# The row sums of a sliding-window softmax issued directly behind their exponential, with the filler units behind them

## The chip, the cores and the metric

The kernel runs on one core of one Trainium2 chip. The metric is device time in microseconds (us); lower is better. A core has five engines that work side by side, each through its own instructions in the order in which they were issued: PE multiplies matrices into PSUM, the accumulators; ACT evaluates functions element by element and here also moves most PSUM results to SBUF (an eviction); DVE does elementwise arithmetic; POOL and SP mostly start transfers. An engine that waits holds up all that is queued behind.

## The reference, cut to what matters

Two independent computations, put side by side in the output. Part A is attention in which each of 2048 positions sees only eight others (itself and every second one of the 15 before it), with 32 heads of 18 channels:

```python
qkv = (x @ wqkv).reshape(B, S, 3, H, Dh)           # S = 2048, H = 32, Dh = 18
idx = pos[:, None] - arange(8)[None, :] * 2        # eight keys for each position
logits = einsum("bhsd,bhswd->bhsw", q, kg) * Dh ** -0.5
logits = where(idx >= 0, logits, -1e9)
attn = softmax(logits, axis=-1)                    # over the eight
o = einsum("bhsw,bhswd->bhsd", attn, vg)
a = o.reshape(B, S, D) @ wo                        # D = 576
```

Part B is a long causal convolution over the 2048 positions for each of 576 channels (in the reference by FFT), of a four-tap filtered `k` times `v`, gated by `q`:

```python
kv = k_shift * v
y = irfft(rfft(pad(kv)) * rfft(pad(ssm_k)))[:S] + kv * ssm_D
b = q * y
out = concatenate([a, b], axis=-1)
```

## The kernel before, in words

Part B is computed as block transforms with matrices of sines and cosines on PE: `mirror` and `fold_filter` prepare blocks, `filter_spectrum` (tile `ps_fk`, lines 627 and 628, evicted by ACT at line 695) transforms the filter, `x_spectrum` (`ps_fx`, line 776, evicted at 778) the signal, and `spectral` multiplies spectra on DVE (line 1099), sums them (`ps_z`, line 1126) and transforms back (`ps_inv`, `ps_back`).

Part A projects `x` to q, k and v (`project`, tile `ps_proj`: lines 378, 382 and 389 on PE, evicted at line 414), in units that are cut in two halves of four matmuls with 512 columns and, in one of the halves, two or four shorter ones at line 382 or 389. `logits` forms products q times k on DVE (line 832) and sums each head's channels on PE (`ps_log`, line 847). `softmax` treats one half of the positions at a time, `hh` 0 and 1, over a tile `at` of 128 partitions and 8 x 256 elements. `weigh` then multiplies by v on DVE (line 956; three buffers take turns, two halves of `av` and a stretch of `qk`) and sums the eight terms on PE with an identity (`ps_acc`, lines 973 and 987), evicted at lines 977 and 991. `output` multiplies by wo (`ps_wo`, lines 1021 and 1029).

PSUM is used as four double banks: two under tag A, two under tag B. A matmul that starts a new tile waits until ACT has evicted the one that used the bank before.

One pass of `softmax` has these steps: maximum over the eight on DVE (lines 875 to 878), subtraction (879), the exponential of all 128 x 2048 elements on ACT (881), the sum over the eight on PE by eight matmuls with the identity into `ps_tot` (887), the reciprocal on ACT as exp(-ln(sum)) (888 and 889), and the multiplication by it on DVE (892). It is a Python generator. Between its yields the caller issues steps of others, so the yields fix what is issued in between on every engine.

Independent PE work lies in a list, `units`. `until()` takes from it the next number in the table `PLACES` and issues so many units at that point of the program; these are the fillers. The sequence of calls to `until()` pairs each call with its number. In the pass for `hh` 0 the call at line 884 issues one unit of `filter_spectrum`; in the pass for `hh` 1 it issues three half units of the v projection, 16 matmuls. The call at line 880 stands ahead of the exponential. The line numbers 885 to 889 of before are lower by one in the changed kernel: 886 is the sum, 887 the logarithm, 888 the second exponential.

Of the kernel before, what the change touches and what calls it, by code (L numbers as in the profile page):

```python
# [53 lines left out]
def view(t, offset, dims):  # L54

    return bass.AP(tensor=t.tensor, offset=t.offset + offset, ap=[list(t.ap[0])] + [list(d) for d in dims])
# [3 lines left out]
def kernel(  # L60
# [58 lines left out]
    def bank2(name, tag):  # L119
        return pp.tile([128, 2, 512], FP32, name=name, tag=tag)  # L120
# [206 lines left out]
    def dve(n, fn, ready=0.0, ns=0.53):  # L327

        fn()
        clk["D"] = max(clk["D"], ready) + n * ns / 1000 + 0.125  # L330
        return clk["D"]

    def pe(us, tag, evac, ready=0.0, first=True, last=True):

        clk["P"] = max(clk["P"], ready, psum[tag].popleft() if first else 0.0) + us
        clk["A"] = max(clk["A"], clk["P"] + 0.1) + evac
        if last:
            psum[tag].append(clk["A"])
        return clk["A"]

    def pop(n=0):
        f = units[n][1]
        del units[n]
        f()
# [3 lines left out]
    def until():  # L348

        for _ in range(next(places, 0)):  # L350
            if units:
                p = max(clk["P"], psum["A"][0] if psum["A"] else 0.0)
                pop(next((n for n, u in enumerate(units) if len(u) < 4 or u[3] <= p), 0))
# [511 lines left out]
    def softmax(hh, big, small):  # L865

        at = attn[hh]
        t4 = view(big, 0, [[256, 4], [1, 256]])
        t2 = view(small, 0, [[256, 2], [1, 256]])
        top = view(big, 0, [[1, 256]])  # L870
        total = view(big, 0, [[1, 512]]).bitcast(FP32)
        part = view(small, 0, [[1, 256]])
        tt = nc.vector.tensor_tensor
        if hh == 0:
            dve(128, lambda: tt(at[0:32, :, 0:PAD], at[0:32, :, 0:PAD], maskb[:], ALU.add), clk["A"])
        dve(1024, lambda: tt(t4, at[:, 0:4, :], at[:, 4:8, :], ALU.max), clk["A"])
        dve(512, lambda: tt(t2, t4[:, 0:2, :], t4[:, 2:4, :], ALU.max))
        dve(256, lambda: tt(top, t2[:, 0, :], t2[:, 1, :], ALU.max))
        r = dve(2048, lambda: tt(at, at, top.unsqueeze(1).to_broadcast([128, W, 256]), ALU.subtract))
        until()  # L880
        nc.scalar.activation(at, at, ACT.Exp, scale=SCALE)
        clk["A"] = max(clk["A"], r) + 1.9
        yield clk["A"]
        until()
        ps = bank2("ps_tot", "B")
        for w in range(W):
            nc.tensor.matmul(ps[:, 0, 0:256], ident[:], at[:, w, :], start=(w == 0), stop=(w == W - 1))
        nc.scalar.activation(total, ps[:, 0, 0:256], ACT.Ln)
        nc.scalar.activation(part, total, ACT.Exp, scale=-1.0)
        pe(0.85, "B", 0.75, clk["A"])  # L890
        yield clk["A"]
        r = dve(2048, lambda: tt(at, at, part.unsqueeze(1).to_broadcast([128, W, 256]), ALU.mult), clk["A"])
        yield r
# [13 lines left out]
    la, lb = logits(0), logits(1)  # L907
    logits_run[0] = True
    sa = softmax(0, view(av, 2048, [[1, 1024]]), view(av, 3072, [[1, 512]]))
    order = [la] * 3 + [partial(negate, 1, 0)] + [la] * 7 + [lb, sa, lb, lb, lb, sa, lb, sa]  # L910
    for n, step in enumerate(order):
# [3 lines left out]
        step() if callable(step) else next(step, None)  # L915
    need("fk0")
    sb_ = softmax(1, view(xw, 11 * HB + D, [[1, 1024]]), view(xw, 11 * HB + D + 1024, [[1, 512]]))


# [426 lines left out]
```

## Time and profile before

| | |
|---|---|
| time before, median of 3 runs (lowest to highest) | 212.2 us (212.09 to 212.56) |
| the profiled execution | 212.5 us |
| its span, first to last instruction | 210.8 us |
| busy: PE, DVE, ACT, POOL | 200.1, 193.1, 150.5, 74.0 us |
| mean granted clock of PE | 0.998 of full speed |

The profile comes from one execution. A row of the view in order of time has the start in us from the span's start, the duration, the engine, the source line, the operation, out<-in by the program's names, the shape, and how many instructions the row holds; in square brackets stand the engine's idle time just before it and what ended it ("issue" where nothing shown did). A row of the chain of waits has start, duration, engine, tile and line. A row by stretches has the stretch, its length, busy us and number of instructions of PE, weight loads, DVE, ACT and POOL, the granted clock, the share of the transfer engines and GB/s. A few matmul records can be missing.

### The profile page before, as it was taken

Reading aid. Unit: us, or ns where it says so; the run is one execution under the profiler, and the core shown is the slowest. Engines: PE = TensorE matmul, PEld = TensorE weight load, DVE = VectorE, ACT = ScalarE, POOL = GpSimd, SP = SyncE. Lnnn points to the kernel's source line nnn. Section 1 sums busy time; section 2 is a strip of 40 time slices with the busy share of each in tenths; the row PEclk is TensorE's granted clock in tenths of the full one; section 3 lists DMA queues with packets and bytes.
Section 4 is the critical chain, followed back from the end, with each engine's and each line's share of the span. In section 5 each row is a group of like instructions: output and inputs, shape, how many; then the busy total and the mean of one; then the engine's idle time right before and its main releaser. Section 6 shows DMA issues by size and latency. Waiting matters only on the chain.

```text
span 210.8 us, 5106 instructions
## 1 busy us (share of the span) xinstructions
PE 200.1 (95%) x2114; PEld 110.7 (53%) x2122; DVE 193.1 (92%) x146; ACT 150.5 (71%) x218; POOL 74.0 (35%) x111
## 2 busy tenths in 40 slices
PE   7999999999999999899999999999989999999891
PEld 2443443344554656564354666656555666666460
DVE  7989999999999999858889999999999849999981
ACT  3799988657684989986369788855666796775540
POOL 8999993001195516320175000002029004033000
PEclk9999999999999999999999999999999999999999
DMA  6999998999639336999999997587559995985133
GB/s 201 303 328 231 266 342 280 170 192 182 151 75 122 48 40 87 180 181 171 235 225 238 194 234 159 105 208 185 153 223 255 239 322 110 214 243 182 28 113 111
DMA packets 35396, 39.66 MB, mean 188 GB/s; under 512 B 17619, under 2 KB 29007, under 8 KB 35374
## 3 DMA queue, kind: packets, MB, share of 16 engines
q1 hardware_dynamic: 26812, 24.88, 47.2%
q0 software_dynamic: 6096, 11.96, 30.4%
q10 hardware_dynamic: 2466, 2.51, 3.5%
q8 instruction: 16, 0.26, 0.5%
q14 instruction: 6, 0.05, 0.1%
HBM read 13.11 MB, written 4.72 MB: 85 GB/s over the span
## 4 chain that ended last, share of the span: by engine, by line
PE 80%; ACT 10%; DVE 5%; issue 2%; DVEq 0%; ACTq 0%
PE ps_proj L378 16%; PE ps_z L1126 9%; PE ps_wo L1029 8%; PE ps_acc L973 7%; PE ps_inv L1158 7%; PE ps_fx L776 6%; PE ps_log L847 4%; PE ps_proj L500 3%; PE ps_fk L627 3%; PE ps_proj L382 3%; PE ps_proj L389 3%; ACT Ks L695 3%; PE ps_rev L673 2%; PE ps_fk L628 1%; ACT qk L977 1%
## 5 line engine op out<-in xcount | busy, mean ns | idle before, releaser
L378 PE MATMUL ps_proj<-xw 128*128 128x512 bf16 x153 | 37.4, 380 | 0.6 <-issue 0.3
L832 DVE TENSOR_TENSOR av<-qk 128x4096 bf16<-128x4096 bf16 (+1 forms) x16 | 31.7, 2013 | 2.8 <-PE ps_log L847 2.8
L378 PEld LDWEIGHTS <-xw 128*128 128x128 bf16 x160 | 14.0, 97 | 20.5 <-issue 6.2
L1099 DVE TENSOR_TENSOR qk<-xw,Ks 128x2304 bf16<-128x2304 bf16 x14 | 18.5, 1355 | 2.5 <-PE ps_inv L1158 2.4
L1139 ACT ACTIVATE av<-ps_z 128x768 bf16<-128x768 f32 x20 | 15.3, 808 | 6.2 <-PE ps_z L1126 6.2
L414 ACT ACTIVATE qk<-ps_proj 128x1024 bf16<-128x1024 f32 x14 | 14.3, 1023 | 7.6 <-PE ps_proj L389 3.3
L695 ACT ACTIVATE Ks<-ps_fk 128x576 bf16<-128x576 f32 x32 | 18.6, 717 | 1.3 <-PE ps_fk L628 1.3
L577 DVE TENSOR_TENSOR tB<-kj,skb 128x4608 bf16<-128x4608 bf16 (+1 forms) x8 | 19.3, 2417 | 0.1
L778 ACT ACTIVATE xw<-ps_fx 128x576 bf16<-128x576 f32 x32 | 18.4, 666 | 0.0
L776 PE MATMUL ps_fx<-xw,TB 128*128 128x288 bf16 x128 | 18.0, 286 | 0.2
L1055 POOL DMA_DIRECT2D Ks<-Ks x3 | 3.7, 1218 | 41.1 <-PE ps_wo L1029 28.7
L1029 PE MATMUL ps_wo<-qk 128*128 128x288 bf16 x128 | 17.8, 287 | 0.0
L627 PE MATMUL ps_fk<-Ks,TB 128*128 128x384 bf16 x62 | 16.9, 326 | 0.8 <-ACT Ks L695 0.7
L414 ACT ACTIVATE v<-ps_proj 128x1024 bf16<-128x1024 f32 x9 | 9.3, 1029 | 9.3 <-PE ps_proj L378 4.3
L973 PE MATMUL ps_acc<-av,ident 64*64 64x512 bf16 x160 | 15.3, 377 | 0.0
L628 PE MATMUL ps_fk<-Ks,TB 128*128 128x192 bf16 x62 | 15.2, 245 | 0.0
L776 PEld LDWEIGHTS <-TB 128*128 128x128 bf16 x128 | 12.0, 97 | 6.0 <-issue 2.9
L1029 PEld LDWEIGHTS <-qk 128*128 128x128 bf16 x128 | 11.6, 98 | 5.6 <-issue 3.0
L1158 PE MATMUL ps_inv<-av,TI 128*128 128x288 bf16 (+1 forms) x96 | 13.6, 293 | 0.6 <-ACT av L1139 0.6
L1161 ACT ACTIVATE v<-ps_inv 128x576 bf16<-128x576 f32 (+1 forms) x14 | 9.5, 677 | 6.3 <-PE ps_inv L1158 6.3
L977 ACT ACTIVATE qk<-ps_acc 128x1024 bf16<-128x1024 f32 x8 | 8.2, 1024 | 8.0 <-PE ps_acc L973 8.0
L956 DVE TENSOR_TENSOR av<-Ks,v 128x4096 bf16<-128x4096 bf16 x6 | 13.6, 2286 | 0.2 <-PE ps_acc L973 0.2
(199 smaller groups left out, 471.3 us busy)
## 6 DMA issues: line engine op xcount, KB each, us to landing
Ks<-Ks POOLq DMA_DIRECT2D x9, 576.0 KB, 7.1
TB<-av SPq DMA_DIRECT2D x12, 256.0 KB, 5.5
kj<-in_B_k_dram SPq DMA_DIRECT2D x6, 504.0 KB, 6.1
vt<-in_B_v_dram SPq DMA_DIRECT2D x8, 288.0 KB, 5.2
Ks<-av SPq DMA_DIRECT2D x8, 256.0 KB, 5.5
Ks<-Ks SPq DMA_DIRECT2D x3, 576.0 KB, 6.1
Ks<-in_A_x_dram SPq DMA_DIRECT2D x2, 576.0 KB, 5.2
xw<-in_A_wqkv_dram SPq DMA_DIRECT2D x2, 576.0 KB, 5.9
```

Source lines behind the costliest of these rows:

```text
L378: nc.tensor.matmul(ps[:, jp, :], wq(kb, comp, 128 * ct, 128), xT(kb, 1024 * jj + 512 * jp, 512), **se)
L414: nc.scalar.activation(view(t, o + pad + 1024 * jj, [[512, 2], [1, 512]]), ps[:], ACT.Copy)
L577: dve(2304 * n, lambda: nc.vector.tensor_tensor(to, view(kj, row * D, [[D, n], [D, 4], [1, D]]), view(skb, row * D, [[D, n], [0, 4], [1, D ...
L627: nc.tensor.matmul(o[:, 0:2], w, rhs[:, 0:2], start=start, stop=stop)
L695: nc.scalar.activation(view(Ks, k_at(m, cs ^ (m & 1)) + 96 * gi, [[768, 3], [384, 2], [1, 96]]), acc3(ps), ACT.Copy, scale=(PSG, MSG)[cs][ ...
L776: nc.tensor.matmul(ps[:, pm, 0:HD], TX[:, 2 * pm + c, 128 * gi:128 * gi + 128], kv[:, 2 * c + pm, HD * h:HD * h + HD], start=(c == 0), sto ...
L832: return P, at, step, dve(1024 * nj, lambda: nc.vector.tensor_tensor(view(P, at, [[step, 4], [256, nj], [1, 256]]), view(t, o + 256 * hh, ...
L973: nc.tensor.matmul(acc[64 * o:64 * o + 64, h, :], ident[64 * h:64 * h + 64, 64 * h:64 * h + 64], view(P, 256 * u, [[2048, 2], [1, 256]])[6 ...
L1029: nc.tensor.matmul(ps[:, r, 0:HD], oT(hh, 2 * c + r, t)[:, o:o + 128], wo[:, t // 2, t % 2, HD * h:HD * h + HD], start=(t == 0 and h == 0) ...
L1099: r = dve(3 * QTR, lambda: nc.vector.tensor_tensor(pr, view(xw, HB * XG[i] + QTR * t, [[HB, 3], [1, QTR]]), view(Ks, k_at(j - i, 0) + QTR ...
L1126: nc.tensor.matmul(view(acc[r], 512 * h, [[192, 2], [96, 2], [1, 96]])[o:o + 64], w[64 * h:64 * h + 64, 64 * h:64 * h + 64], pr[64 * h:64 ...
L1158: nc.tensor.matmul(ps[:, c, 0:n], TI[:, sl, pm, 128 * c:128 * c + 128], Y(j, pm)[:, sl, c0:c0 + n], start=(pm == 0 and sl == 0), stop=(sl ...
```

## The change

`until()` moves from ahead of the sums to behind the reciprocal; the yield that follows it stays.

```diff
         nc.scalar.activation(at, at, ACT.Exp, scale=SCALE)
         clk["A"] = max(clk["A"], r) + 1.9
         yield clk["A"]
-        until()
         ps = bank2("ps_tot", "B")
         for w in range(W):
             nc.tensor.matmul(ps[:, 0, 0:256], ident[:], at[:, w, :], start=(w == 0), stop=(w == W - 1))
         nc.scalar.activation(total, ps[:, 0, 0:256], ACT.Ln)
         nc.scalar.activation(part, total, ACT.Exp, scale=-1.0)
         pe(0.85, "B", 0.75, clk["A"])
+        until()
         yield clk["A"]
```

The instructions are the same, and so is their number. Their order changes on PE and ACT alone. On ACT both passes show in the difference of the two programs; the first piece is the pass for `hh` 0, where line 887 and 888 of the change are the logarithm and the second exponential, line 881 the exponential over the eight, 695 and 778 evictions of the spectra, and x8 means eight in a row:

```order
 L695 ACTIVATE Ks<-ps_fk 128x6x96 x5
 L881 ACTIVATE av<-av 128x2048
-L695 ACTIVATE Ks<-ps_fk 128x6x96 x9
-L888 ACTIVATE av<-ps_tot 128x256
-L889 ACTIVATE av<-av 128x256
-L695 ACTIVATE Ks<-ps_fk 128x6x96 x3
+L695 ACTIVATE Ks<-ps_fk 128x6x96 x8
+L887 ACTIVATE av<-ps_tot 128x256
+L888 ACTIVATE av<-av 128x256
+L695 ACTIVATE Ks<-ps_fk 128x6x96 x4
```

One eviction of `ps_fk` has moved behind the two activations. The second piece, on ACT too, is the pass for `hh` 1, where 414 are the evictions of the v projection, 991 and 977 those of the weighted sums:

```order
 L991 ACTIVATE qk<-ps_acc 128x512
 L881 ACTIVATE av<-av 128x2048
+L887 ACTIVATE xw<-ps_tot 128x256
+L888 ACTIVATE xw<-xw 128x256
 L414 ACTIVATE v<-ps_proj 128x1024 x2
-L888 ACTIVATE xw<-ps_tot 128x256
-L889 ACTIVATE xw<-xw 128x256
 L977 ACTIVATE qk<-ps_acc 128x1024
```

Two evictions of the projection now stand behind the logarithm instead of ahead of it. On PE the pass for `hh` 1 was as follows, from the end of line 987's sums to the start of line 973's; the numbers behind names tell tiles apart, and what an instruction waits for stands in brackets:

```order
L987 MATMUL ps_acc_1401<-av_782,ident_98 64x256
L378 LDWEIGHTS xw_63
L378 MATMUL ps_proj_1439<-xw_63 128x512 [waits Activation_49]
...
L389 MATMUL ps_proj_1439<-xw_63 128x512
...
L389 MATMUL ps_proj_1454<-xw_63 128x512 [waits Activation_49]
...
L378 MATMUL ps_proj_1454<-xw_63 128x512
L887 LDWEIGHTS ident_98
L887 MATMUL ps_tot_1466<-av_782,ident_98 128x256 [waits Activation_49]
...
L973 LDWEIGHTS ident_98 [waits DVE_49]
L973 MATMUL ps_acc_1477<-av_782,ident_98 64x512 [waits PE_49]
```

With the change the same stretch of PE reads:

```order
L987 MATMUL ps_acc_1401<-av_782,ident_98 64x256
L378 LDWEIGHTS xw_63
L378 MATMUL ps_proj_1439<-xw_63 128x512 [waits Activation_49]
...
L886 LDWEIGHTS ident_98 [waits PE_49]
L886 MATMUL ps_tot_1447<-av_782,ident_98 128x256 [waits Activation_49]
...
L389 MATMUL ps_proj_1439<-xw_63 128x512
...
L389 MATMUL ps_proj_1465<-xw_63 128x512 [waits PE_49]
...
L378 MATMUL ps_proj_1465<-xw_63 128x512
L973 LDWEIGHTS ident_98 [waits DVE_49]
L973 MATMUL ps_acc_1477<-av_782,ident_98 64x512 [waits PE_49]
```

Between line 987 and the sums there were 20 matmuls of the projection (16 of line 378 and four of line 389); now there are four of line 378, and the other 16 stand behind the sums. The sums' first matmul waits for the exponential on ACT in both programs.

## The prediction

> **What bounds the kernel now.** I read the page's busy shares first, then the chain of work that ended last, then the order of time on single engines around the two softmax passes. The page (the span, busy times and shares, the chain by engine):
>
> ```profile
> span 210.8 us, 5106 instructions
> PE 200.1 (95%) x2114; PEld 110.7 (53%) x2122; DVE 193.1 (92%) x146; ACT 150.5 (71%) x218; POOL 74.0 (35%) x111
> PE 80%; ACT 10%; DVE 5%; issue 2%; DVEq 0%; ACTq 0%
> ```
>
> PE and DVE are both nearly full, and 80% of the chain is PE. So the question is which of the two waits for the other. DVE alone, in order of time (start, duration, then idle time before it and what ended it), and one line of the view by stretches of time:
>
> ```profile
> 93.27 1.23 DVE L892 TENSOR_TENSOR av<-av 128x2048 bf16<-128x2048 bf16 x1 [1.74 <-ACT av L889]
> ...
> 97.45 4.49 DVE L832 TENSOR_TENSOR av<-qk 128x4096 bf16<-128x4096 bf16 x2 [0.75 <-PE ps_log L847]
> 102.63 3.43 DVE L832 TENSOR_TENSOR av<-qk 128x4096 bf16<-128x4096 bf16 x2 [0.69 <-PE ps_log L847]
> 106.68 2.29 DVE L956 TENSOR_TENSOR av<-TB,v 128x4096 bf16<-128x4096 bf16 x1 [0.62 <-PE ps_log L847]
> ...
> 115.94 2.28 DVE L956 TENSOR_TENSOR av<-Ks,v 128x4096 bf16<-128x4096 bf16 x1
> 118.15 1.22 DVE L892 TENSOR_TENSOR av<-av,xw 128x2048 bf16<-128x2048 bf16 x1
> 119.28 2.28 DVE L956 TENSOR_TENSOR av<-Ks,v 128x4096 bf16<-128x4096 bf16 x1
> ...
> 170.28 1.36 DVE L1099 TENSOR_TENSOR qk<-xw,Ks 128x2304 bf16<-128x2304 bf16 x1 [2.40 <-PE ps_inv L1158]
> ...
> 174.22 1.36 DVE L1099 TENSOR_TENSOR v<-xw,Ks 128x2304 bf16<-128x2304 bf16 x1 [1.30 <-PE ps_wo L1021]
> ```
> ```profile
> 174.00:202.00 28.00, 27.09 (x444) 17.75 (x440) 27.79 (x22) 17.17 (x27) 6.26 (x8) 1.00 0.58 145
> ```
>
> The reader is to see the direction: from 97 to 174 us every marked wait of DVE is ended by PE (0.75, 0.69, 0.62, 2.40, 1.30 us). PE sets the pace up to 174 us; from the release at 174.22 DVE works almost without a gap (27.79 of 28.00 us). Time lost on PE before 174 therefore moves the end; time won on DVE before 174 only lengthens its next wait.
>
> **The change, part by part.** Nothing is added or removed. At each of the two softmax passes the eight sum matmuls move ahead of fillers on PE, and the logarithm and the second exponential move ahead of these fillers' evictions on ACT. DVE, POOL and SP keep their order, so no transfer is moved past another one.
>
> *First pass: one unit of the filter spectrum stood ahead of the sums.* ACT, then PE, alone:
>
> ```profile
> 86.29 4.56 ACT L695 ACTIVATE Ks<-ps_fk 128x576 bf16<-128x576 f32 x8
> 91.53 0.65 ACT L695 ACTIVATE Ks<-ps_fk 128x576 bf16<-128x576 f32 x1 [0.68 <-PE ps_fk L628]
> 92.41 0.38 ACT L888 ACTIVATE av<-ps_tot 128x256 f32<-128x256 f32 x1 [0.22 <-PE ps_tot L887]
> 92.82 0.42 ACT L889 ACTIVATE av<-av 128x256 bf16<-128x256 f32 x1
> 93.14 1.71 ACT L695 ACTIVATE Ks<-ps_fk 128x576 bf16<-128x576 f32 x3
> ```
> ```profile
> 90.83 0.34 PE L627 MATMUL ps_fk<-Ks,TB 128*128 128x384 bf16 x1
> ...
> 91.33 1.04 PE L887 MATMUL ps_tot<-av,ident 128*128 128x256 bf16 x8
> 92.21 0.33 PE L627 MATMUL ps_fk<-xw,TB 128*128 128x384 bf16 x1
> ...
> 92.84 0.32 PE L627 MATMUL ps_fk<-xw,TB 128*128 128x384 bf16 x1
> ```
>
> The unit takes 91.33 - 90.83 = 0.50 us of PE. The sums need the bank that the last of the eight evictions reads (end 86.29 + 4.56 = 90.85), and PE takes up a freed bank 0.05 us after ACT's end (92.41 + 0.38 = 92.79, next matmul 92.84). They start at 90.90 instead of 91.33, a gain of 0.43 us; the logarithm, 1.08 us behind the first sum (92.41 - 91.33), starts at 91.98, and line 892 on DVE at 92.84. That 0.43 us lies off the path: DVE's next wait grows from 0.75 to about 1.18 us, since PE does not hurry.
>
> What PE pays there: the moved unit's eviction now stands behind both activations. It starts at 91.98 + (93.14 - 92.41) = 92.71 and ends 0.65 later, at 93.36; the third unit behind it uses the same bank. It could start at 90.90 + 0.88 for the sums (92.21 - 91.33) + three units of 0.50 = 93.28, and waits until 93.41, 0.13 us. In exchange the 0.13 us disappears that PE now loses at 92.84, where it waits for the logarithm to free its bank (it could start at 92.21 + 0.50 = 92.71). The evictions and the units behind run at the same pace of about 0.55 us, so a little of the lag stays. I bound this term by -0.1 (the wait goes, the other is hidden) and +0.2 us (two such waits) and take +0.1, since the ACT queue ends its four evictions later than its three before.
>
> *Second pass: three half units of the v projection (16 matmuls) stood ahead of the sums.* The chain of waits here, then PE alone, then ACT alone:
>
> ```profile
> 111.12 1.00 PE ps_acc L987 x32
> 112.12 0.32 PE ps_proj L378
> ...
> 116.32 0.87 PE ps_tot L887 x8
> 117.19 1.91 PE ps_acc L973 x32
> ...
> 121.83 1.92 PE ps_acc L973 x32
> ```
> ```profile
> 112.05 1.90 PE L378 MATMUL ps_proj<-xw 128*128 128x512 bf16 x7
> 113.88 0.61 PE L389 MATMUL ps_proj<-xw 64*128 64x512 bf16 x4
> ...
> 116.16 1.04 PE L887 MATMUL ps_tot<-av,ident 128*128 128x256 bf16 x8
> ```
> ```profile
> 112.24 0.64 ACT L991 ACTIVATE qk<-ps_acc 128x512 bf16<-128x512 f32 x1
> 112.72 1.95 ACT L881 ACTIVATE av<-av 128x2048 bf16<-128x2048 bf16 x1
> ...
> 116.36 1.02 ACT L414 ACTIVATE v<-ps_proj 128x1024 bf16<-128x1024 f32 x1 [0.77 <-PE ps_proj L378]
> 117.28 0.38 ACT L888 ACTIVATE xw<-ps_tot 128x256 f32<-128x256 f32 x1
> 117.69 0.42 ACT L889 ACTIVATE xw<-xw 128x256 bf16<-128x256 f32 x1
> ```
>
> Here the big exponential is what counts: it runs on ACT from 112.72 to 114.67, behind the eviction at 112.24, which itself waits for the sums of line 987. Before, PE had 16 matmuls more to do and came to the sums at 116.16, 1.5 us after the exponential's end. Now only four matmuls lie between line 987 and the sums. Eight of them (one record is missing) take 113.88 - 112.05 = 1.83 us, four 0.92 us, so PE is there at 112.97 and can start at 114.67 + 0.05 = 114.72: **PE stands still for 1.75 us**. All 16 matmuls that would have covered it are queued behind. Bounds: by the chain's times, where the same matmuls run from 112.12, PE is ready at 113.04 and the wait is 1.67; if the weights for the first sum aren't loaded ahead, at most 0.1 more, 1.85. I take 1.75, by the starts.
>
> Who waits for that: line 973 starts at 117.19 + 1.75 = 118.94 and ends 1.91 later, at 120.85 instead of 119.10. DVE's product at 119.28 overwrites the half of av that line 973 reads; DVE, which came to it at 119.28 without a wait, now waits until 120.9, some 1.6 us. That product ends at 120.9 + 2.3 = 123.2, before the second line 973 wants it (121.83 + 1.75 = 123.6), so DVE adds nothing of its own. ACT's two projection evictions now stand behind the logarithm; the later one starts when the 16th matmul ends, 118.94, takes 1.02 and is out of the way at 119.96, before line 973 ends and is evicted.
>
> What is won here: the logarithm is done earlier by 116.16 - 114.72 = 1.44 us, and the reciprocal by 116.7. But line 892 stands on DVE behind the product that ends at 115.94 + 2.28 = 118.22 and starts at 118.15 as before. The gain is nothing.
>
> **Sum**: +0.1 and +1.75 = +1.85 us on PE, all of it ahead of the point at 174 us where PE releases DVE. The profiled execution took 212.5 us (span 210.8, 1.7 around it), 0.3 over the median of 212.2; against it the sum gives 214.35, and against the median 212.2 + 1.85 = 214.05, rounded to 214.0 us.
>
> **Rivals.** *The clock falls in the new gap.* The stretches behind the last matmul (the first pair of numbers is PE's: no work) show what idling does to the granted clock, the third number from the right:
>
> ```profile
> 206.20:208.00 1.80, 0.00 (x0) 0.00 (x0) 1.01 (x2) 0.00 (x0) 0.00 (x0) 1.00 0.58 158
> 208.00:209.50 1.50, 0.00 (x0) 0.00 (x0) 0.00 (x0) 0.00 (x0) 0.00 (x0) 1.00 0.31 73
> 209.50:210.80 1.30, 0.00 (x0) 0.00 (x0) 0.00 (x0) 0.00 (x0) 0.00 (x0) 0.64 0.00 0
> ```
>
> PE is idle for 3.3 us at full clock, and only then it falls. A gap of 1.75 us is half of that, so I hold it for safe. Did it fall all the same, and stay low for as long as it took to fall, at half speed, PE would lose another 3.3 / 2 = 1.65 us: 215.7. Half speed and that length are assumptions of mine. The Trainium skill, "TensorE: Matmul & The Clock Gate", in the section "Why this matters for your kernels", warns of idle gaps of PE above about 3 us and of half speed after one window of them. By that rule 1.75 us costs no clock, which the three rows bear out; by a shorter window this rival would hold.
>
> *A part of the stall comes back at a later wait of PE.* The largest wait of PE behind the place, PE alone:
>
> ```profile
> 153.36 0.36 PE L1126 MATMUL ps_z<-Ks,ident 64*64 64x384 bf16 x4 [0.83 <-ACT qk L977]
> ```
>
> If what ends it were not moved by the stall, up to 0.83 us would return: 214.05 - 0.83 = 213.2. Against it: this eviction follows a line 973 on PE, so it moves with PE.
>
> *Faster: DVE sets the pace.* The place is line 892 of the first pass, the price the 0.43 us that it starts earlier: 212.2 - 0.43 = 211.8. It decides if PE has at least 1.75 us of slack at line 973, so that the stall costs nothing, and if DVE's waits for PE are not real. DVE's 92% speak for it; against it stand the five waits above, all ended by PE, and that line 973 follows the sums without a gap (116.32 + 0.87 = 117.19). With the slack but without DVE in the lead the time stays at 212.2.
>
> **How the numbers follow.** Forecast 0.84, part of it back 0.08, clock 0.03, no change 0.03, faster 0.02. Less than 0.2%, 0.4 us, can't be told from no change; the forecast, the part and the clock are all slower: 0.95 against 0.03 and 0.02. The range goes down to the case of a part given back with the low term at the first pass (213.2 less 0.1, 213.1), and up to the high terms, 212.2 + 0.2 + 1.85, with the 0.4 that the runs spread upward: 214.7.
>
> **What would show it.** In the profile after: a wait of PE of about 1.7 us at line 886, ended by ACT line 881, near 114.7 us; a wait of DVE of about 1.6 us near 119.3, ended by PE line 973; line 892 near 92.8 in the first pass with DVE's wait before it down to 1.3 us, and its next wait up to 1.2; line 892 of the second pass hardly moved; the first DVE line 1099 after the long wait near 172. I am wrong if PE's wait is there but line 973 starts near 117, or if the end moves less than PE does at 120 us.

## The result and the profile after

The changed kernel takes 214.44 us (median of 4 runs, 213.97 to 215.55), before 212.22 (212.09 to 212.56). The ratio is 1.0104, with a 95% interval of 1.0072 to 1.0136. It is slower by 2.2 us by the medians and by 1.9 us by the lowest times. The forecast was 214.0 us, with a range of 213.1 to 214.7.

The profiled execution of the changed kernel is the longest of its four, 215.55 us. Its page and its chain, then the longest wait of PE in the view of waits (who waited for whom, us in total, times, longest):

```profile
span 213.8 us, 5106 instructions
PE 201.7 (94%) x2114; PEld 111.6 (52%) x2122; DVE 193.4 (90%) x146; ACT 150.6 (70%) x218; POOL 73.8 (35%) x111
PE 73%; ACT 10%; DMA 8%; SPq 3%; issue 2%; DVE 1%; POOL 0%; DVEq 0%; ACTq 0%
```
```profile
PE ps_tot L886 <- ACT av L881: 1.6, 1, 1.6
```

Nothing was added, and the engines wait longer: the busy times of DVE, ACT and POOL differ by 0.3 us at most from before, that of PE by 1.6, with a few of its records missing in both. The wait of PE that stands first here did not exist before. Its place in the order of time, PE alone and then ACT alone, second softmax pass:

```profile
113.68 1.04 PE L378 MATMUL ps_proj<-xw 128*128 128x512 bf16 x3
116.35 1.03 PE L886 MATMUL ps_tot<-av,ident 128*128 128x256 bf16 x8 [1.64 <-ACT av L881]
117.22 1.03 PE L378 MATMUL ps_proj<-xw 128*128 128x512 bf16 x4
118.18 0.61 PE L389 MATMUL ps_proj<-xw 64*128 64x512 bf16 x4
118.72 1.90 PE L378 MATMUL ps_proj<-xw 128*128 128x512 bf16 x8
120.55 0.40 PE L973 MATMUL ps_acc<-av,ident 64*64 64x512 bf16 x2
```
```profile
113.87 0.64 ACT L991 ACTIVATE qk<-ps_acc 128x512 bf16<-128x512 f32 x1
114.35 1.95 ACT L881 ACTIVATE av<-av 128x2048 bf16<-128x2048 bf16 x1
117.42 0.38 ACT L887 ACTIVATE xw<-ps_tot 128x256 f32<-128x256 f32 x1 [1.12 <-PE ps_tot L886]
118.62 1.02 ACT L414 ACTIVATE v<-ps_proj 128x1024 bf16<-128x1024 f32 x1 [0.36 <-PE ps_proj L389]
```

The exponential ends at 114.35 + 1.95 = 116.30 and the sums start at 116.35, 0.05 later. If the four matmuls take the 0.92 us that the prediction gave them, the sums could have started at 114.60, and PE stands still for 1.75 us by the starts; the profile's own idle time is 1.64. The 16 matmuls that did this time's work before now follow. The first pass, PE and ACT, and a row of the kernel before for comparison:

```profile
92.43 1.03 PE L886 MATMUL ps_tot<-av,ident 128*128 128x256 bf16 x8
...
94.92 0.32 PE L627 MATMUL ps_fk<-Ks,TB 128*128 128x384 bf16 x1
...
95.46 1.73 PE L776 MATMUL ps_fx<-xw,TB 128*128 128x288 bf16 x12
```
```profile
87.82 4.56 ACT L695 ACTIVATE Ks<-ps_fk 128x576 bf16<-128x576 f32 x8
93.50 0.38 ACT L887 ACTIVATE av<-ps_tot 128x256 f32<-128x256 f32 x1 [1.12 <-PE ps_tot L886]
93.91 0.42 ACT L888 ACTIVATE av<-av 128x256 bf16<-128x256 f32 x1
94.24 2.25 ACT L695 ACTIVATE Ks<-ps_fk 128x576 bf16<-128x576 f32 x4
```
```profile
93.83 1.73 PE L776 MATMUL ps_fx<-xw,TB 128*128 128x288 bf16 x12
```

The eight evictions start 1.53 us later than before (87.82 against 86.29), in work that stands ahead of the change. The row of line 776 starts 1.63 later (95.46 against 93.83). So the first pass itself costs PE 0.10 us. DVE, alone:

```profile
94.36 1.23 DVE L892 TENSOR_TENSOR av<-av 128x2048 bf16<-128x2048 bf16 x1 [1.31 <-ACT av L888]
99.08 4.49 DVE L832 TENSOR_TENSOR av<-qk 128x4096 bf16<-128x4096 bf16 x2 [1.29 <-PE ps_log L847]
...
119.78 1.22 DVE L892 TENSOR_TENSOR av<-av,xw 128x2048 bf16<-128x2048 bf16 x1
122.51 2.29 DVE L956 TENSOR_TENSOR av<-Ks,v 128x4096 bf16<-128x4096 bf16 x1 [1.52 <-PE ps_acc L973]
...
172.43 1.36 DVE L1099 TENSOR_TENSOR qk<-xw,Ks 128x2304 bf16<-128x2304 bf16 x1 [0.75 <-PE ps_z L1126]
...
176.15 1.36 DVE L1099 TENSOR_TENSOR v<-xw,Ks 128x2304 bf16<-128x2304 bf16 x1 [1.08 <-DMA xw<-xw]
```

The wait ahead of the first line 892 has shrunk from 1.74 to 1.31 us and the next has grown from 0.75 to 1.29: what the earlier reciprocal gained was waited away at once. At 122.51 the new wait on line 973 appears. The last two rows don't fit the prediction: the wait at 176.15 is ended by a transfer, and both rows are only about 2 us later than before, although PE is 3.4 us later by then: 1.63 at the first matmuls of line 378 (113.68 against 112.05) and 1.75 of stall.

Why this execution was late at 84 us already shows in its chain of waits ahead of the change:

```profile
45.15 6.06 SPq L227
51.26 8.34 DMA Ks<-in_B_ssm_k_dram
...
66.33 3.35 DMA Ks<-Ks
```

The transposing load of the filter and the transfers behind it ended last there, before the change takes effect.

### The profile page after: what moved, and what is told of

The parts are those of the page before. It is cut to its first block, busy times and chain, and to the rows that moved or that the text cites. A ratio compares the mean times of both kernels' runs of the same rounds, so it can differ in the third digit from the quotient of the medians.

```text
span 213.8 us, 5106 instructions
## 1 busy us (share of the span) xinstructions
PE 201.7 (94%) x2114; PEld 111.6 (52%) x2122; DVE 193.4 (90%) x146; ACT 150.6 (70%) x218; POOL 73.8 (35%) x111
## 4 chain that ended last, share of the span: by engine, by line
PE 73%; ACT 10%; DMA 8%; SPq 3%; issue 2%; DVE 1%; POOL 0%; DVEq 0%; ACTq 0%
PE ps_proj L378 13%; PE ps_z L1126 9%; PE ps_wo L1029 8%; PE ps_inv L1158 7%; PE ps_acc L973 7%; PE ps_fx L776 5%; DMA Ks<-in_B_ssm_k_dram 4%; PE ps_proj L500 3%; SPq L227 3%; DMA Ks<-Ks 3%; PE ps_fk L627 3%; PE ps_log L847 3%; ACT Ks L695 2%; PE ps_proj L389 2%; ACT av L881 2%
```

## The experiments

Three theories go through the experiments. A: PE's lag is the cause, but 0.4 us of it is given back at the end, where PE waited for DVE before (the spans differ by less than PE's lag in the middle). B: all of PE's lag reaches the end, as the prediction had it. C: the lateness ahead of the change belongs to the changed program. All times below are in us. The kernel before ran beside all of them: lowest 212.06 or 212.07, median 212.10 to 212.15. Most scatter goes upward; so the lowest time stands beside the median.

| kernel | lowest | median | ratio to before (95%) |
|---|---|---|---|
| changed, again | 213.99 | 214.16 | 1.0083 (1.0052 to 1.0113) |
| first pass alone | 212.18 | 212.30 | 0.9996 (0.9973 to 1.0019) |
| second pass alone | 213.87 | 214.05 | 1.0079 (1.0047 to 1.0110) |
| before, 8 more matmuls | 213.80 | 213.92 | 1.0103 (1.0057 to 1.0149) |
| before, 2 more matmuls | 212.50 | 212.84 | 1.0025 (1.0015 to 1.0034) |
| second pass, one half unit ahead | 212.79 | 212.90 | 1.0043 (1.0020 to 1.0066) |
| second pass, two half units ahead | 212.06 | 212.37 | 1.0005 (0.9995 to 1.0016) |
| changed, half an exponential | 213.12 | 213.40 | 1.0053 (1.0039 to 1.0068) |
| before, spectra's transfers first | 212.07 | 212.53 | 1.0025 (0.9995 to 1.0055) |
| changed, spectra's transfers first | 213.98 | 214.15 | 1.0087 (1.0055 to 1.0119) |

**The changed kernel again.** No edit.

> The changed kernel once more. Its profiled execution was already 1.5 us late at the first softmax pass, in work that stands ahead of the change. Theory A (the stall of PE at line 886 costs 1.75 us, about 0.1 is added at the first pass, and 0.4 us is given back at the end because before PE waited there for DVE): about 1.45 us more than before, 213.6 to 213.8, and the lateness at 84 us comes and goes between executions. Theory B (all of PE's lag reaches the end, as the prediction had it): 1.85 us more, 214.0. Theory C (the lateness ahead of the change belongs to the changed program): at least 2.2 us more, 214.4 or above.

DVE's second pass and its release, then PE, in this execution:

```profile
121.09 2.29 DVE L956 TENSOR_TENSOR av<-Ks,v 128x4096 bf16<-128x4096 bf16 x1 [1.51 <-PE ps_acc L973]
...
175.18 1.36 DVE L1099 TENSOR_TENSOR v<-xw,Ks 128x2304 bf16<-128x2304 bf16 x1 [0.81 <-DMA xw<-xw]
183.43 2.63 DVE L1099 TENSOR_TENSOR qk<-xw,Ks 128x2304 bf16<-128x2304 bf16 x2 [0.55 <-PE ps_z L1126]
```
```profile
111.26 1.07 PE L987 MATMUL ps_acc<-av,ident 64*64 64x256 bf16 x32
...
114.93 1.03 PE L886 MATMUL ps_tot<-av,ident 128*128 128x256 bf16 x8 [1.63 <-ACT av L881]
...
119.13 0.40 PE L973 MATMUL ps_acc<-av,ident 64*64 64x512 bf16 x2
```

The same two ends of the stretch in the kernel before:

```profile
111.05 1.07 PE L987 MATMUL ps_acc<-av,ident 64*64 64x256 bf16 x32
...
117.12 0.40 PE L973 MATMUL ps_acc<-av,ident 64*64 64x512 bf16 x2
```

From line 987 to line 973 PE needs 7.87 us here and 6.07 before: 1.80 more. This distance leaves out what happened ahead of the change; it is compared with the time in all the runs that follow.

Without the lateness at the start (the stall at 114.93 lies where the prediction put it, 114.7) the kernel takes 213.99 to 214.34, lowest 1.93 above before's lowest. Theory C falls: the lateness comes and goes, and the profile of the kernel before with two more matmuls has it too (its eight evictions of line 695 start at 87.56 instead of 86.29). A falls too; B, the prediction's sum of 1.85, stands.

**First pass alone**, and **second pass alone**: `until()` stands behind the reciprocal for one `hh` and ahead of the sums for the other.

```diff
-        until()
+        if hh == 1:
+            until()
         ps = bank2("ps_tot", "B")
...
         pe(0.85, "B", 0.75, clk["A"])
+        if hh == 0:
+            until()
```

> The sums go ahead of the filler in the first softmax pass alone; the second pass is as before. Prediction: line 892 starts about 0.4 us earlier against line 881, DVE's next wait grows by as much, PE loses 0 to 0.2 us, time 212.2 to 212.4. Rival (DVE sets the pace): 211.8.

> The sums go ahead of the fillers in the second softmax pass alone; the first pass is as before. PE waits about 1.7 us for line 881. Theory A (0.4 us given back at the end): 1.35 us more than before, 213.5. Theory B (all of the lag reaches the end): 1.75 more, 213.95. If the first pass were the cause: 212.2.

DVE of the first-pass kernel (the edit moves the multiplication to line 895):

```profile
92.83 1.23 DVE L895 TENSOR_TENSOR av<-av 128x2048 bf16<-128x2048 bf16 x1 [1.31 <-ACT av L890]
97.55 4.49 DVE L832 TENSOR_TENSOR av<-qk 128x4096 bf16<-128x4096 bf16 x2 [1.29 <-PE ps_log L847]
```

The multiplication starts at 92.83 instead of 93.27, and the next wait is 1.29 instead of 0.75 us. The lowest time rises by 0.12; it does not fall by 0.4: DVE does not set the pace here. The second pass alone raises the lowest by 1.81. The two parts, 0.12 and 1.81, add up to the 1.93 of the whole.

**Eight, or two, more matmuls on PE at the place of the stall**, in the kernel before. The first matmul of the half unit behind line 987 is issued 8 (or 2) times more; its result is overwritten.

```diff
                 if ct < 4:
+                    for _ in range(8 if (comp, jj, ct, jp, kb) == (2, 1, 2, 0, 0) else 0): nc.tensor.matmul(...)
                     nc.tensor.matmul(ps[:, jp, :], wq(kb, comp, 128 * ct, 128), xT(kb, 1024 * jj + 512 * jp, 512), **se)
```

> The kernel before with eight more matmuls of 512 columns on PE at the place of the stall, behind line 987 (the first matmul of that half unit is repeated; the result is overwritten and the output stays the same). PE is held up by 1.83 us of work instead of by a wait. Theory A: 1.4 us more than before, 213.6. Theory B: 1.8 more, 214.0. Rival of the falling clock: clearly less than the second pass alone, since PE never idles here.

> The kernel before with two more matmuls of 512 columns at the place of the stall, 0.46 us of PE. Theory B: 0.46 us more, 212.55. Theory A (0.4 us of slack at the end): 212.15.

PE with eight more matmuls, from line 987 to line 973:

```profile
111.15 1.07 PE L987 MATMUL ps_acc<-av,ident 64*64 64x256 bf16 x32
...
118.95 0.40 PE L973 MATMUL ps_acc<-av,ident 64*64 64x512 bf16 x2
```

That is 7.80 us, 1.73 more than before (not the 1.83 expected), all of it work, and the lowest time rises by 1.74. In the second pass alone the distance is 7.87, 1.80 more, by idling, and the lowest time rises by 1.81. So an idle time of this length has no price of its own. Two more matmuls lengthen the distance by 0.44 us and the lowest time by 0.43. So in the fastest runs there is no slack on PE behind this place, not even 0.4 us. The granted clock (the third number from the right, stretches of the changed kernel's second execution) says the same of the idle time:

```profile
112.00:116.00 4.00, 2.37 (x26) 1.34 (x18) 4.00 (x2) 2.88 (x4) 1.99 (x2) 1.00 1.08 228
116.00:120.00 4.00, 4.00 (x32) 1.50 (x34) 3.57 (x3) 2.59 (x4) 0.00 (x0) 1.00 1.08 202
```

The idle time lies in the first, and the clock is full in both.

**One, or two, of the three half units ahead of the sums** in the second pass (the first pass as before):

```diff
-        until()
+        fillers = next(places, 0)
+        until(1 if hh else fillers)
         ps = bank2("ps_tot", "B")
...
         pe(0.85, "B", 0.75, clk["A"])
+        if hh:
+            until(fillers - 1)
```

> Second pass alone, with one of the three half units ahead of the sums and two behind. PE has six matmuls more to do before it comes to the sums, until about 114.15 us, so its wait for line 881 is 0.55 us instead of 1.7. Theory B (PE's lag reaches the end undiminished): 0.55 us more than before, 212.65. Theory A (0.4 us of any lag is given back): 212.25. If the time were lost to anything else that the new order brings, it would stay near 214.0.

> Second pass alone, with two of the three half units ahead of the sums and one behind. PE comes to the sums at about 115.3 us, after the exponential's end, so it doesn't wait; the reciprocal is done 0.8 us earlier than before. Theory B: 212.1, as before. If an earlier reciprocal were worth something: down to 211.3. If the order itself cost time: above 212.5.

The sums on PE, with one half unit ahead and with two:

```profile
114.51 0.39 PE L389 MATMUL ps_proj<-xw 64*128 64x512 bf16 x2
115.35 1.03 PE L888 MATMUL ps_tot<-av,ident 128*128 128x256 bf16 x8 [0.45 <-ACT av L881]
116.32 0.39 PE L389 MATMUL ps_proj<-xw 64*128 64x512 bf16 x2
```
```profile
115.58 1.04 PE L888 MATMUL ps_tot<-av,ident 128*128 128x256 bf16 x8
```

With one half unit PE waits 0.45 us by its idle time, 0.52 by the starts, and the lowest time is 0.72 up, 0.2 more than expected; the stretch from line 987's to line 973's first matmul grew by 0.72 too (111.68 to 118.47). The other 0.20 us can be read off the starts. The sums now stand between two pairs of matmuls of line 389, which has 64 rows where its neighbours have 128. A pair takes 0.32 us to the next start (116.32 to 116.64), two of them 0.64, where all four in a row took 0.54 (113.88 to 114.42 before): 0.10 more. The sums and the eight matmuls of line 378 that now end the stretch take 0.97 and 1.83 us, where the same two pieces of work took 0.96 and 1.74 before: 0.10 more. With two half units PE doesn't wait, the distance is 6.08 against 6.07, and the lowest time is that of before. The median is 212.37 against 212.15, and the interval of the ratio holds 1. The reciprocal's lead is worth nothing. The loss of the change is the wait for the exponential; an order that parts like matmuls, as with one half unit, adds 0.1 us at each of the two new seams.

**Half an exponential** in the changed kernel. In the second pass four of the eight keys are not exponentiated; this part of the computation is left out.

```diff
-        nc.scalar.activation(at, at, ACT.Exp, scale=SCALE)
+        some = at[:, 0:4, :] if hh else at
+        nc.scalar.activation(some, some, ACT.Exp, scale=SCALE)
```

> The changed kernel, where the exponential of the second pass is evaluated for four of the eight keys alone (the other four enter the sums as they are, so the output is another). Line 881 takes about 1.0 us there instead of 1.95. If PE's wait is a wait for it, the wait falls from 1.65 to about 0.7 us and the time by 0.95, to 213.1. If PE waits for a bank or for DVE, the time stays near 214.1.

ACT, then PE:

```profile
113.07 1.10 ACT L882 ACTIVATE av<-av 128x1024 bf16<-128x1024 bf16 x1
```
```profile
114.23 1.03 PE L887 MATMUL ps_tot<-av,ident 128*128 128x256 bf16 x8 [0.78 <-ACT av L882]
```

The exponential is 0.85 us shorter (1.10 instead of 1.95), the wait 0.85 (0.78 instead of 1.63) and the lowest time 0.87. So it is this instruction that PE waits for.

**The spectra's transfers ahead of the loads of q**, in the kernel before and in the changed one:

```diff
-    load_q(0)
-    load_q(1)
     for x, n in THIRDS[1]:
         if x:
             need(f"fx{n}")
         third(x, n)
+    load_q(0)
+    load_q(1)
```

> The kernel before, where the transfers of lines 1054 and 1055 for the spectra are queued ahead of the loads of q instead of behind them, with the softmax as before. In the traces so far DVE's line 1099 is released late, at 173.1 to 177.3 us, and the span ends 36.5 us later or more. If that release is by the transfers of line 1055 and not by PE, as the waits named it, it comes some us earlier now, at 172 or before, and the times above the lowest go: median 212.1, the same lowest, 212.06. If PE releases DVE, nothing changes: release at 174, median 212.15 with the same spread.

> The changed kernel with the same transfers queued first. Theory B with this second cause out of the way: the whole of PE's lag, 1.9 us, shows against the kernel above: 214.0, with less spread than the changed kernel's 213.97 to 215.55. If the transfers had a part in the changed kernel's loss: 213.5 or less.

POOL in the kernel before, then POOL and DVE with the new order:

```profile
160.58 1.30 POOL L1055 DMA_DIRECT2D Ks<-Ks  x1
161.34 1.78 POOL L1055 DMA_DIRECT2D xw<-xw  x1
```
```profile
158.87 1.16 POOL L1055 DMA_DIRECT2D Ks<-Ks  x1 [13.94 <-DMA Ks<-Ks]
160.22 1.18 POOL L1055 DMA_DIRECT2D xw<-xw  x1 [0.19 <-issue]
```
```profile
171.96 1.36 DVE L1099 TENSOR_TENSOR v<-xw,Ks 128x2304 bf16<-128x2304 bf16 x1 [1.11 <-PE ps_z L1126]
...
184.35 1.36 DVE L1099 TENSOR_TENSOR av<-xw,Ks 128x2304 bf16<-128x2304 bf16 x1 [0.31 <-DMA Ks<-Ks]
```

The transfers leave POOL 1.1 to 1.7 us earlier, PE's program is the same, and DVE's release moves from 174.22 to 171.96. So a transfer of line 1055 had released it, as the kernel's code allows: the product at that place reads what the transfer adds up. But the times don't improve: the lowest stays at 212.07, and the median, 212.53, isn't told apart from before. In the profiled execution (span 210.8, as before) a later transfer is now waited for (184.35). The changed kernel with the same edit keeps its distance: 213.98, 1.91 above. None of these versions beats the kernel before.

## Why the prediction was right, point by point

**The stall.** PE's wait for line 881 was put at 1.75 us near 114.7. It is 1.75 by the starts if four matmuls take 0.92 us (112.26 to 114.93 in the second execution, and alike in the first), and 1.63 by the idle time in brackets. But line 973 comes 1.80 us later against line 987. The missing 0.05 lies in the 0.92: it is half of a stretch of eight that ends at line 389's smaller matmuls. Eight that lead straight to the sums took 1.74 before (114.42 to 116.16), so four take 0.87, and the wait is 1.80. The time follows this distance in all the experiments: 1.80 more gives 1.81, 1.73 gives 1.74, 0.72 gives 0.72, 0.44 gives 0.43 and 0.01 gives nothing.

**The first pass.** +0.1 us was taken from between -0.1 and +0.2; it measured 0.10 on PE and 0.12 in the lowest time. The wait for the logarithm's bank went, and a wait of about 0.15 for the moved eviction came at the third unit behind it (94.92), as worked out. DVE's wait went from 1.74 to 1.31, as forecast, and the next one to 1.29 instead of 1.18, the 0.1 us that PE lost being added.

**The second line 892** did not move against DVE's products: it follows the product ahead without a wait. DVE's new wait at line 956 was put at 1.6 and is 1.52. ACT's later eviction ends ahead of line 973's, so it hides.

**The sum**, 1.85 us, is 1.93 by the lowest times. The forecast's 214.0 was laid against medians, and the first four runs' median, 214.44, lies 0.4 above it. The profiled one of them, 215.55, was late by transfers ahead of the change; what made the others late no trace shows. The five later runs have a median of 214.16.

**What was wrong in it.** The step "every marked wait of DVE is ended by PE", with the point at 174 us "where PE releases DVE", failed in two of the five waits, and with it the path that was to carry PE's lag to the end. In the kernel before the rows at 170.28 and 174.22 name PE, but in the changed kernel the instruction of the second of them names the transfer `xw<-xw` (176.15); and queueing the transfers earlier took the first wait away and moved the second release by 2.3 us without touching PE.

So there are two limits at the end: PE's own work, and DVE's release plus about 36.5 us (174.22 to the span of 210.8 before; 176.00 to 212.6 in the second pass alone, where the line has the number 1102; 177.26 to 213.8 with eight more matmuls):

```profile
176.00 1.36 DVE L1102 TENSOR_TENSOR v<-xw,Ks 128x2304 bf16<-128x2304 bf16 x1 [1.15 <-PE ps_wo L1024]
```
```profile
177.26 1.36 DVE L1099 TENSOR_TENSOR v<-xw,Ks 128x2304 bf16<-128x2304 bf16 x1 [1.79 <-DMA xw<-xw]
```

The profiles show which one ended last. In seven of the twelve profiles (the changed kernel twice and once more with the transfers first, the first pass alone, two more matmuls, two half units ahead, half an exponential) the span ends 93.25 to 93.28 us behind line 973's first matmul: there PE is the later limit. In the other five it ends later, by 93.68 to 94.85. DVE is the limit there: in four of them the span ends 36.5 to 36.6 us behind the release near 175, in the fifth (before, transfers first) behind the later release at 184.35. Before by PE alone would end at 117.12 + 93.27 = 210.39, and 210.4 is the span of its fastest runs. So in the lowest times PE's own work is the later limit, and the forecast's sum held. In the profiled execution of before (212.5 us, span 210.8) DVE was the later one. That is why the two profiles differ by 3.4 us on PE in the middle and by only 3.0 in the span (213.8 against 210.8), and why theory A looked possible. It is also one of the prediction's own signs of being wrong, "if the end moves less than PE does at 120 us", and what it points at is real: the sum of 1.85 holds against an execution of before that PE ends, and the profiled one, from which it was read, is not one of these. About half of the executions of before are: 34 of the 64 that ran beside the experiments have the span of 210.4. That the sum could be laid against their median is luck as far as the prediction goes.

**The rivals.** The clock did not fall (1.00 in the stretch with the idle time and in the next, and PE held up by work costs as much as PE idle). No part of the stall comes back: 0.44 us of PE costs 0.43, and the wait of PE at line 1126 that the rival named is still 0.83 us in the second execution, 2.01 us later (155.37 against 153.36), as line 973 is. DVE doesn't set the pace: the first pass alone is no gain.

## What to carry to other kernels

A short dependent step that is issued straight behind its producer on another engine makes an in-order engine wait for what is left of the producer; independent work placed between them is not in the way, it is the cover. How much is needed can be read off: the producer's end, less the time at which the waiting engine arrives (here 1.80 us in the second pass, where two of three filler units were enough, and nothing in the first, where the exponential had ended 4 us before). An earlier result is worth something only if its consumer is not queued behind other work: here the consumer stood behind three products in one pass and ran into a wait for PE in the other.

## What the runs showed of the hardware that was not expected

The five accumulating transfers inside SBUF, 576 KB each, issued by POOL at line 1055, took between 5.4 and 14.1 us from issue to landing within one execution (eight more matmuls) and 5.4 to 12.7 in another (before). With the loads of q queued behind them instead of ahead it was 5.6 to 9.2 (before, transfers first). Executions of the kernel before spread from 212.06 to 214.60 us; that some of them end late by such a transfer is shown by the profiles in which DVE is the later limit, how much of the spread it makes is not. And a wait that the profile puts down to PE can be a transfer's: of two executions with the same wait, one named PE and the other the transfer.
